# Splitting the returned denominators on GpSimd ahead of the bulk loads, in a one-core kernel that gates linear attention with a ReGLU block

## The chip, the cores and the metric

The kernel runs on one core of a Trainium2 chip. A core has five engines that run side by side: TensorE (PE in the profile; PEld is its weight load) multiplies matrices into PSUM, VectorE (DVE), ScalarE (ACT) and GpSimd (POOL) work elementwise, and SyncE (SP) issues DMAs. DMAs issued by SP and by GpSimd come from different queues and are carried by the same 16 DMA engines. Engines wait for each other by semaphores, and each engine works through its own instructions in order.

The metric is the device time of one execution in microseconds; lower is better.

## The reference

The output mixes two branches of the same input x (2048 tokens of width 576) by a sigmoid gate. Branch a is linear attention with 32 heads of 18 features, whose feature map is a softmax and a softmax of the negated value. Branch b is a ReGLU feed-forward of width 4608.

```python
q, k, v = x @ wqkv, split into 32 heads
phi(y) = concat(softmax(y @ w_phi), softmax(-(y @ w_phi)))
kv  = einsum("bhsf,bhsd->bhfd", phi(k), v)
z   = einsum("bhsf->bhf", phi(k))
num = einsum("bhqf,bhfd->bhqd", phi(q), kv)
den = einsum("bhqf,bhf->bhq", phi(q), z) + 1e-6
a   = (num / den) @ wo
b   = (relu(x @ W_gate) * (x @ W_up)) @ W_down
out = g * a + (1 - g) * b        # g = sigmoid(x @ gate_w)
```

All of it is fp32. The kernel multiplies in fp32r, a form of lower precision, and makes up for it by splitting operands: the high part is the value copied to fp32r, the low part is the value minus the high part, and a product is taken as high·high, high·low and low·high.

## The kernel before

**Stage 1, up to about 247 us.** The loop over 16 tiles of 128 tokens makes keys, values and queries. `softmax_parts` finds the maxima, exponentials and sums of a tile; `key_steps` and `query_steps` scale it (one half of `e` on DVE, the other on GpSimd, L209). `turn` transposes a tile of queries on PE (tile `ptr`), ACT copies it to `et`, and an SP DMA stores it in DRAM as `eT`; the last four tiles stay on chip. `gate_logits` takes the gate's exponential from a column of the values tile `vt` and then sets 11 columns of it to one by a memset on GpSimd (L295). The matmuls of `kv_step` sum phi(k)ᵀv.

Beside this the loop prepares operands of stage 3. At t = 8 `scaled_sums` begins: it loads four tiles `xb` of 128 × 3 × 512 (L330), multiplies each by the rows `sb` (L333) and forms four differences (L338), all on GpSimd, and SP stores seven results as `xt` (L327). It is a generator, and each turn of the loop takes three steps of it.

**Stage 2, about 247 to 392 us.** The queries are worked through in four blocks of 512 tokens. `BLOCKS = (3, 0, 1, 2)` gives their order, and "block 0" to "block 3" below mean places in it. For each block:

1. `fetch` loads its turned queries into `ph`, four DMAs of 594 KB (L426): blocks 0 and 1 need none or come by SP, blocks 2 and 3 come by GpSimd's queue. Token tiles 10 and 11 belong to block 3, and their `eT` is stored by GpSimd's queue first (L387).
2. `sums` multiplies `ph` by the summed kv (PE, L542), ACT copies the results to `R` and `og`, and small SP DMAs collect the denominators as `dn` (L548, L550).
3. `gather` moves other rows of `og` into `R` by SP DMAs (L561, L564).
4. `invert` takes the reciprocal of `dn` (L579), multiplies it by the gate rows `gT` (L580) and sends it to another layout by an SP DMA, `kt<-dn` (L582), 32 rows of 512.
5. `split_inverse` splits what came back into high and low, the tile `rd`: ACT copies (L588), DVE subtracts (L589).
6. `divide`, once for each of five row groups: PE spreads `rd` over rows by a matmul with the 0/1 matrix `spread` (L600), DVE multiplies `R` by it (L602), ACT and DVE split the result into `oh` and `ol` (L603, L604).
7. `first_out` (block 0) and `project_out` (others) multiply by wo on PE, and `rows_out` copies the rows and stores them (`att`, L755).

`gate_rows` copies the gates to `gx` on GpSimd (L569), transposes them on PE (L573), and ACT copies them to `gT` (L574). `load_operand` issues loads of `xr` by GpSimd's queue for stage 3, and `root_rows` stores `sb` by the same queue (L743).

**Stage 3, from about 392 us.** The feed-forward, with matmuls at L1084, L1124 and L1147. The change does not touch it.

**What sets the order.** Stage 2 is written inside `in_order(tc, nc, nc.tensor, nc.sync, nc.gpsimd)`: PE, SP and GpSimd execute in the order of the code there. DVE and ACT are ordered by the scheduler of the framework, except where `after` holds an instruction behind another. In stage 1 the scheduler orders all engines. Once made, each engine's order is fixed. Tiles come from pools, and a tile that reuses a buffer waits for the last reader of it.

Of the kernel before, what the change touches and what calls it, by code (L numbers as in the profile page):

```python
# [1 line left out]

# [5 lines left out]
F32 = mybir.dt.float32  # L8
# [75 lines left out]
def gated_mix_kernel(  # L84
# [27 lines left out]
    tt = nc.vector.tensor_tensor  # L112
# [180 lines left out]
    def gate_logits(t):  # L293
        nc.scalar.activation(gs[:, t:t + 1], VT[t][:, 0:1], AF.Exp, scale=-1.0)
        nc.gpsimd.memset(VT[t][:, 0:(NQ - 1) * GS + 1:GS], 1.0)  # L295
# [72 lines left out]
    def turn_all(t, bb):  # L368

        for b, ps in bb:  # L370
            for i, g in enumerate(QN[b]):
                nc.tensor.transpose(ps[:, i], flat(EQ[t])[:, QC[g]:QC[g] + QK], ident)  # L372
        for b, ps in bb:
            gg = QN[b]
            if t >= FIRST:
                o = PH[t // 4][:, t % 4]
            else:
                if t not in ET:
                    ET[t] = etp.tile([QK, NQ, P], F32, name="et")
                o = ET[t]  # L380
            nc.scalar.activation(o[:, gg.start:gg.stop], ps[:, :len(gg)], AF.Copy)
        TURNED[t] = TURNED.get(t, 0) + len(bb) - 1
        TURNED[t] = TURNED.get(t, 0) + 1
        if TURNED[t] == 3:
            EQ.pop(t)
            if t < FIRST:
                (nc.sync if t < FIRST - 2 else nc.gpsimd).dma_start(eT[t * QK:(t + 1) * QK], ET.pop(t).rearrange("p g t -> p (g t)"))  # L387
# [54 lines left out]
    xw = AR.enter_context(tc.tile_pool(name="xw", bufs=4, **R_))  # L442
# [13 lines left out]
    for t in range(2, NT - 2):  # L456
        if t in (6, 10):
            load_x(t // 4 + 1)
        if t == 8:
            whole(half_gates(0))  # L460
            sb = xw.tile([P, 2, TB], F32, name="sb", bufs=1)
            for i in range(2):
                on_all_rows(pv1.tile([P, TB], F32, name="pg", tag="pv1"), sb[:, i], i)
            first_half = scaled_sums(nc.gpsimd.tensor_tensor, 0, [xw.tile([P, 3, TB], F32, name="xb") for _ in range(4)], sb, 0, TB)
        for _ in range(3):
            next(first_half, None)
        if t == 12:
# [11 lines left out]
            spread = kt_p.tile([2 * H, 5, P], F32R, name="spread")  # L479
            ones = raw.tile([2 * H, 5, P], F32, name="ones", tag="raw")  # L480
# [73 lines left out]
    RD, OW = {}, {}  # L554
# [21 lines left out]
    def invert(b):  # L576

        dn = DN.pop(b)
        nc.vector.reciprocal(dn, dn)  # L579
        tt(out=dn, in0=gT[:, BLOCKS[b] * P:(BLOCKS[b] + 1) * P], in1=dn, op=MULT)  # L580
        d2 = kt_[:H, :TB]
        nc.sync.dma_start(d2, dn)  # L582

    def split_inverse(b):

        d2 = kt_[:H, :TB]
        rd = RD[b] = rb.tile([2 * H, TB], F32R, name="rd", bufs=1)
        nc.scalar.activation(rd[:H], d2, AF.Copy)  # L588
        tt(out=rd[H:], in0=d2, in1=rd[:H].bitcast(F32), op=SUB)  # L589

    def divide(b, k):
# [7 lines left out]
        ps = kv_bank(1 - k % 2 if b > 1 else 0)  # L599
        nc.tensor.matmul(ps[:n], spread[:, k, :n], RD[b], start=True, stop=True)  # L600
# [47 lines left out]
    with in_order(tc, nc, nc.tensor, nc.sync, nc.gpsimd):  # L648
# [41 lines left out]
        sums(0, (3, 2), (two[:, 0], two[:, 1]))  # L690
        sums(0, (1,), (kv_bank(2),))
# [3 lines left out]
        turn(FIRST - 2, 0, turned(kv_bank(0)))  # L695
        turn(FIRST - 2, 1, turned(kv_bank(1)))
        turn(FIRST - 2, 2, turned(kv_bank(0)))
# [10 lines left out]
        with after(tc, nc, nc.scalar, last_of(nc, nc.scalar)):  # L708
            split_inverse(0)
# [8 lines left out]
        gather(1, 4, 3, 2, 1, 0)  # L718
# [105 lines left out]
    pt = nc.gpsimd.tensor_tensor  # L824
# [85 lines left out]
    with in_order(tc, nc, nc.tensor, nc.sync, nc.gpsimd):  # L910
        x0, x1, x2 = (operand_ahead(i) for i in range(3))
        load_operand(0, 0, nc.gpsimd)
        load_operand(0, 1, nc.gpsimd)
        fetch(BLOCKS[3], nc.gpsimd)
# [8 lines left out]
        divide(1, 4)  # L923
        for m in range(5):
            first_out(0, (m,))
            rows_out(0, m, PW[m])
            if m == 1:
                divide(1, 3)
            if m == 3:
                divide(1, 2)  # L930
        sums(2, (1, 0), halves)
        gather(2, 4, 3, 2, 1, 0)
        divide(1, 1)
        divide(1, 0)
        for m in range(5):
# [4 lines left out]
            if m == 2:  # L940
                gather(3, 4, 3, 2, 1, 0)
            if m == 0:
                invert(2)
                split_inverse(2)
            else:
# [3 lines left out]
            if m == 2:  # L949
                whole(x0)  # L950
            if m == 4:
                divide(2, 0)
                invert(3)
                split_inverse(3)
# [569 lines left out]
def _layout(A_x, A_wqkv, A_w_phi, A_wo, B_W_gate, B_W_up, B_W_down, gate_w):  # L1524
# [33 lines left out]
    spread = np.zeros((2, H, 5, P), np.float32)  # L1558
# [8 lines left out]
    spread = spread.reshape(2 * H, 5, P)  # L1567
# [19 lines left out]
```

## Time and profile before

| | us |
|---|---|
| median of 3 runs (lowest to highest) | 1648.82 (1646.73 to 1649.28) |
| profiled execution | 1647.01 |
| its span, first to last instruction | 1644.9 |
| TensorE busy in it | 1592.0 |
| mean granted TensorE clock | 0.986 of full speed |

The profiled execution is one run with the hardware profiler. Its span is 2.1 us shorter than the time of that execution, and that time lies 1.8 us below the median of the runs. Rows of the profile name an instruction by engine, line, operation and tiles, written as output<-inputs; a line can be that of a helper. The view of waits lists who waited for whom: the total, how often, and the longest. "x4" at the end of a row is a count. In the timeline the first number is the start and the second the duration, and a bracket gives the idle time ahead of the instruction and what ended it. In the chain of waits each piece is the work or the transfer that the next step had to wait for.

### The profile page before, as it was taken

How to read it: one execution, taken by the hardware profiler on the slowest of the kernel's cores; microseconds unless marked ns; L12 is line 12 of the kernel's file. 1: busy time of each engine (PE TensorE's matmuls, PEld its weight loads, DVE VectorE, ACT ScalarE, POOL GpSimd, SP SyncE). 2: the span in 40 equal slices, each digit the busy share in tenths (PEclk: the TensorE clock that was granted, in tenths of full speed). 3: DMA queues.
4: the chain of work that ended last, by engine and by line, in shares of the span. 5: the costliest groups of instructions: out<-in, count | busy, mean ns of one | idle time of the engine just before them, and what ended most of it. 6: DMA issues, size and time to landing. Idle time of an engine off the chain costs nothing.

```text
span 1644.9 us, 20158 instructions
## 1 busy us (share of the span) xinstructions
PE 1592.0 (97%) x7823; PEld 1322.1 (80%) x7823; DVE 1198.4 (73%) x1852; ACT 562.9 (34%) x922; POOL 163.9 (10%) x234
## 2 busy tenths in 40 slices
PE   9998997788999999999999999999999999999998
PEld 8898995456888888888888887778888888888887
DVE  4998674356778777887777778667777677777777
ACT  4344334345333333333233234223232323223231
POOL 0128211000000000000000002111111111111110
PEclk9999998899999999999999999999999999999999
DMA  8154305527775566565554543554343434344342
GB/s 265 65 180 165 113 17 146 147 90 289 282 255 204 200 233 240 204 219 208 216 203 184 198 161 115 170 211 165 133 175 133 191 127 178 131 164 159 143 166 72
DMA packets 65306, 284.42 MB, mean 173 GB/s; under 512 B 6842, under 2 KB 17338, under 8 KB 56508
## 3 DMA queue, kind: packets, MB, share of 16 engines
q1 hardware_dynamic: 62764, 273.14, 45.6%
q0 software_dynamic: 1872, 8.97, 2.0%
q8 instruction: 61, 1.00, 0.2%
q10 hardware_dynamic: 576, 1.05, 0.2%
q14 instruction: 33, 0.27, 0.0%
HBM read 172.51 MB, written 109.21 MB: 171 GB/s over the span
## 4 chain that ended last, share of the span: by engine, by line
PE 84%; DVE 5%; DMA 5%; ACT 2%; issue 2%; SPq 1%; POOL 1%; POOLq 0%; ACTq 0%; DVEq 0%
PE cx L1084 27%; PE ca L1084 13%; PE pd L1124 12%; PE pd L1147 10%; PE cy L1084 7%; PE kv L175 2%; PE pq L175 2%; PE pm L1124 2%; PE pm L1147 2%; PE pk L175 2%; DMA kt<-dn 2%; DMA wdr<-wd 1%; DVE sm L204 1%; PE pv L237 1%; PE ptr L372 1%
## 5 line engine op out<-in xcount | busy, mean ns | idle before, releaser
L1191 ACT ACTIVATE hh<-g 128x512 fp32r<-128x512 f32 x195 | 120.2, 626 | 459.1 <-DVE g L1241 289.8
L1162 DVE TENSOR_TENSOR ac<-pd,ac 128x512 f32<-128x512 f32 x238 | 164.1, 689 | 145.4 <-PE pd L1147 145.3
L1084 PE MATMUL cx<-xo,wb 128*128 128x512 f32 x1008 | 250.9, 392 | 4.6 <-DVE u L1366 3.5
L1084 PE MATMUL cx<-xo,ws 128*128 128x512 f32 x1008 | 252.4, 390 | 2.9 <-ACT g L1245 2.1
L1084 PE MATMUL ca<-xo,ws 128*128 128x512 f32 x1008 | 252.0, 389 | 0.6 <-DMA ws<-wsd 0.6
L1084 PEld LDWEIGHTS cx<-xo,wb 128*128 128x128 f32 x1008 | 189.1, 189 | 46.8 <-DVE u L1366 4.3
L1084 PEld LDWEIGHTS cx<-xo,ws 128*128 128x128 f32 x1008 | 188.9, 188 | 43.7 <-ACT g L1245 3.4
L1084 PEld LDWEIGHTS ca<-xo,ws 128*128 128x128 f32 x1008 | 189.1, 188 | 40.3 <-issue 1.0
L1124 PE MATMUL pd<-hh,wd 128*128 128x512 f32 x576 | 200.7, 389 | 0.0
L1147 PE MATMUL pd<-hh,wd 128*128 128x512 f32 x476 | 185.2, 389 | 0.0
L1130 DVE TENSOR_TENSOR ac<-pd,ac 128x512 f32<-128x512 f32 x144 | 99.1, 688 | 105.4 <-PE pd L1124 102.9
L1196 DVE TENSOR_TENSOR hl<-g,hh 128x512 fp32r<-128x512 f32 x195 | 136.5, 700 | 1.9 <-ACT hh L1191 0.2
L1245 ACT ACTIVATE g<-cx 128x512 f32<-128x512 f32 x144 | 85.0, 590 | 128.0 <-PE cx L1084 127.9
L1124 PEld LDWEIGHTS pd<-hh,wd 128*128 128x128 f32 x576 | 108.1, 188 | 22.5
L1084 PE MATMUL cy<-xo,wb 128*128 128x512 f32 x504 | 125.9, 389 | 0.0
L1047 ACT ACTIVATE wd<-wdr 128x384 fp32r<-128x384 f32 (+1 forms) x106 | 62.3, 606 | 152.6 <-DMA wdr<-wd 152.6
L1124 PE MATMUL pd<-hl,wd 128*128 128x512 f32 x288 | 112.1, 389 | 1.0 <-ACT xo L810 1.0
L1084 PEld LDWEIGHTS cy<-xo,wb 128*128 128x128 f32 x504 | 94.6, 188 | 19.6
L1147 PEld LDWEIGHTS pd<-hh,wd 128*128 128x128 f32 x476 | 89.4, 188 | 18.6
L1147 PE MATMUL pd<-hl,wd 128*128 128x512 f32 x238 | 92.6, 389 | 0.0
L794 POOL TENSOR_TENSOR xo<-xr,xo 32x512 fp32r<-32x512 f32 x5 | 8.2, 1653 | 664.8 <-DVE xo L794 657.1
L1050 DVE TENSOR_TENSOR wd<-wdr,wd 128x384 fp32r<-128x384 f32 (+1 forms) x106 | 69.5, 670 | 5.5 <-ACT wd L1047 5.5
(248 smaller groups left out, 2586.3 us busy)
## 6 DMA issues: line engine op xcount, KB each, us to landing
wsd<-ws SPq DMA_DIRECT2D x34, 1280.0 KB
ws<-wsd SPq DMA_DIRECT2D x34, 1280.0 KB
wbd<-wb SPq DMA_DIRECT2D x34, 960.0 KB
wb<-wbd SPq DMA_DIRECT2D x34, 960.0 KB
wr<-wgu SPq DMA_DIRECT2D x36, 768.0 KB
wdr<-wd SPq DMA_DIRECT2D x36, 576.0 KB
eT<-et SPq DMA_DIRECT2D x10, 594.0 KB
xt<-xb SPq DMA_DIRECT2D x7, 768.0 KB
```

Source lines behind the costliest of these rows:

```text
L175: nc.tensor.matmul(ps, w, m, start=i == 0, stop=i == len(pairs) - 1)
L204: nc.vector.tensor_reduce(out=sm.rearrange("p h s -> p (h s)"), in_=e.rearrange("p h s f -> p (h s) f"), axis=AX, op=ADD)
L1047: nc.scalar.activation(o[:, 0], a, AF.Copy)
L1050: tt(out=o[:, 1], in0=a, in1=o[:, 0].bitcast(F32), op=SUB)
L1084: nc.tensor.matmul(ps, w, v, start=first and m == 0, stop=m == len(pairs) - 1, skip_group_check=True)
L1124: nc.tensor.matmul(ps, w, v, start=k == 0 and (i < 2 or first), stop=k == len(mms) - 1 and (i < 2 or last), skip_group_check=True)
L1130: tt(out=a, in0=ps, in1=a, op=ADD)
L1147: mm = lambda ps, w, v, a, z: nc.tensor.matmul(ps, w, v, start=a, stop=z, skip_group_check=True)
L1162: tt(out=a, in0=ps, in1=a, op=ADD)
L1191: nc.scalar.activation(h, src, AF.Copy)
L1196: tt(out=l, in0=src, in1=h.bitcast(F32), op=SUB)
L1245: nc.scalar.activation(a, ps, AF.Copy)
```

## The change

The change has these parts:

- **Halves.** `scaled_sums` for the first half of the tokens is made in two parts of 256 columns, with eight half tiles `xb` of 128 × 3 × 256, and each turn of the loop takes five steps instead of three.
- **Memset.** The memset of `vt` in `gate_logits` goes from GpSimd to DVE.
- **Gate rows.** `gate_rows` stands between the sums of block 0, ahead of the last turns of token tile 10, which now use three banks at once.
- **Return first.** `split_inverse` runs on GpSimd (a copy and a subtraction). The store of the turned queries of tiles 10 and 11, the `fetch` of blocks 2 and 3 and the operand loads stand in GpSimd's code after a split.
- **Place of the inversions.** Each `invert` stands right after the first gather (`gather(b, 4)`), the other gathers after it; `invert(1)` moves up from the fourth sum of block 2 to the third division of block 0, and blocks 2 and 3 move up likewise.
- **Upper partitions.** Blocks 1 and 3 use partitions 64 to 127 of `kt`, `rd` and `spread` (128 rows now, the 0/1 matrix four times), blocks 0 and 2 the lower ones. There is one tile `rd` for all.
- **Banks.** `project_out` alternates two PSUM banks over blocks 1 and 2 and four banks in block 3; two divisions of block 1 alternate banks.

```diff
-        nc.gpsimd.memset(VT[t][:, 0:(NQ - 1) * GS + 1:GS], 1.0)
+        nc.vector.memset(VT[t][:, 0:(NQ - 1) * GS + 1:GS], 1.0)
...
-            if t < FIRST:
-                (nc.sync if t < FIRST - 2 else nc.gpsimd).dma_start(eT[...], ET.pop(t)...)
+            if t < FIRST - 2:
+                store_turned(t, nc.sync)
...
-            first_half = scaled_sums(nc.gpsimd.tensor_tensor, 0, [xw.tile([P, 3, TB], F32, name="xb") for _ in range(4)], sb, 0, TB)
-        for _ in range(3):
+            halves = [[xw.tile([P, 3, TB // 2], F32, name="xb") for _ in range(4)] for _ in range(2)]
+            first_half = chain(*(scaled_sums(pt, 0, halves[c], sb[:, :, c * TB // 2:][:, :, :TB // 2], c * TB // 2, TB // 2)
+                                 for c in range(2)))
+        for _ in range(5):
...
     def invert(b):
         dn = DN.pop(b)
         nc.vector.reciprocal(dn, dn)
         tt(out=dn, in0=gT[:, BLOCKS[b] * P:(BLOCKS[b] + 1) * P], in1=dn, op=MULT)
-        d2 = kt_[:H, :TB]
-        nc.sync.dma_start(d2, dn)
+        nc.sync.dma_start(kt_[2 * H * (b % 2):][:H, :TB], dn)
 
     def split_inverse(b):
-        d2 = kt_[:H, :TB]
-        rd = RD[b] = rb.tile([2 * H, TB], F32R, name="rd", bufs=1)
-        nc.scalar.activation(rd[:H], d2, AF.Copy)
-        tt(out=rd[H:], in0=d2, in1=rd[:H].bitcast(F32), op=SUB)
+        if not RD:
+            RD.append(rb.tile([4 * H, TB], F32R, name="rd", bufs=1))
+        i = 2 * H * (b % 2)
+        d2, hi, lo = kt_[i:i + H, :TB], RD[0][i:i + H], RD[0][i + H:i + 2 * H]
+        nc.gpsimd.tensor_copy(hi, d2)
+        pt(out=lo, in0=d2, in1=hi.bitcast(F32), op=SUB)
...
         sums(0, (3, 2), (two[:, 0], two[:, 1]))
+        gate_rows()
         sums(0, (1,), (kv_bank(2),))
...
-        gate_rows()
-        fetch(BLOCKS[2], nc.gpsimd)
         final = query_steps(FIRST - 1, eng=nc.vector)
         next(final)
-        gather(0, 4, 3, 2)
+        gather(0, 4)
         invert(0)
-        gather(0, 1, 0)
+        gather(0, 3, 2, 1, 0)
+        split_inverse(0)
+        store_turned(FIRST - 2, nc.gpsimd)
+        fetch(BLOCKS[2], nc.gpsimd)
...
         divide(0, 2)
+        gather(1, 4)
+        with after(tc, nc, nc.vector, last_of(nc, nc.vector)):
+            invert(1)
+        gather(1, 3, 2, 1, 0)
+        split_inverse(1)
...
+        store_turned(FIRST - 1, nc.gpsimd)
         divide(0, 1)
...
+        fetch(BLOCKS[3], nc.gpsimd)
         load_operand(0, 0, nc.gpsimd)
         load_operand(0, 1, nc.gpsimd)
-        fetch(BLOCKS[3], nc.gpsimd)
         first_out(2, range(5))
         sums(2, (4, 5), halves)
         divide(0, 0)
-        invert(1)
-        split_inverse(1)
...
-        gather(2, 4, 3, 2, 1, 0)
+        gather(2, 4)
+        invert(2)
+        gather(2, 3, 2, 1, 0)
+        split_inverse(2)
...
-    ps = kv_bank(2) if m % 2 else pv1.tile([P, TB], F32, name="pw", tag="pv1")
+    i = 5 * (b - 1) + m + 1
+    i = i % 2 if b < 3 else i % 4
+    ps = pv1.tile([P, TB], F32, name="pw", tag="pv1") if i == 0 else kv_bank((2, 0, 1)[i - 1])
```

Three places show how the order of instructions moves. The first is GpSimd in stage 1, around the scaled operands: `xb` are the operands, `e` the softmax tiles that GpSimd scales, `r` and `sm` the factors of queries and keys. Before:

```order
L333 TENSOR_TENSOR xb<-xb,sb 128x1536 x3
L209 TENSOR_TENSOR e<-e,r 128x32x18
L333 TENSOR_TENSOR xb<-xb,sb 128x1536
L295 MEMSET vt 128x11
L338 TENSOR_TENSOR xb<-xb 128x1536 x2
L209 TENSOR_TENSOR e<-e,sm 128x32x18
L338 TENSOR_TENSOR xb<-xb 128x1536 x2
L209 TENSOR_TENSOR e<-e,r 128x32x18
```

After:

```order
L334 TENSOR_TENSOR xb<-xb,sb 128x768 x5
L210 TENSOR_TENSOR e<-e,r 128x32x18
L339 TENSOR_TENSOR xb<-xb 128x768
L334 TENSOR_TENSOR xb<-xb,sb 128x768
L339 TENSOR_TENSOR xb<-xb 128x768
L334 TENSOR_TENSOR xb<-xb,sb 128x768
L339 TENSOR_TENSOR xb<-xb 128x768
L334 TENSOR_TENSOR xb<-xb,sb 128x768
L210 TENSOR_TENSOR e<-e,sm 128x32x18
L339 TENSOR_TENSOR xb<-xb 128x768 x3
L210 TENSOR_TENSOR e<-e,r 128x32x18
L339 TENSOR_TENSOR xb<-xb 128x768 x2
```

Ahead of the second query scale (the second row with `r`) stood eight full passes; now fourteen half passes stand there, and two follow it.

The second place is GpSimd in stage 2, from the copy of the gates on. Before:

```order
L387 DMA eT<-et 108x1408
L569 COPY gx<-gates 128x512
L426 DMA ph<-eT 108x1408 x4
L387 DMA eT<-et 108x1408
L769 DMA xr<-xt 128x1536 x2
L426 DMA ph<-eT 108x1408 x4
L743 DMA sbd<-sb 128x512 x2
L769 DMA xr<-xt 128x1536
```

After:

```order
L575 COPY gx<-gates 128x512
L595 CAST rd<-kt 32x512
L596 TENSOR_TENSOR rd<-kt,rd 32x512
L391 DMA eT<-et 108x1408
L430 DMA ph<-eT 108x1408 x4
L595 CAST rd<-kt 32x512
L596 TENSOR_TENSOR rd<-kt,rd 32x512
L391 DMA eT<-et 108x1408
L430 DMA ph<-eT 108x1408 x4
```

The two pairs of `rd` rows are the splits of blocks 0 and 1; each waits for its `kt<-dn`, and the store and the bulk load come behind it. The operand loads follow the second bulk load, then the splits of blocks 2 and 3 with the stores of `sb` between them.

The third is SP at the second return. Before, `kt<-dn` of block 1 stood behind rows of block 2:

```order
L561 DMA R<-og 20x512 x4
L548 DMA dn<-og 24x1x128
L550 DMA dn<-R 8x1x128
L582 DMA kt<-dn 32x4x128
L548 DMA dn<-R 24x1x128 x2
```

After:

```order
L554 DMA dn<-R 24x1x128 x4
L570 DMA R<-og 14x512 x2
L587 DMA kt<-dn 32x4x128
L567 DMA R<-og 20x512 x4
L554 DMA dn<-og 24x1x128
```

It now stands ahead of four gathers of its own block and of all rows of block 2.

More of the change, by code (lines that the diff above doesn't have):

```diff
@@ L1 @@
 from contextlib import ExitStack, contextmanager
+from itertools import chain
 import concourse.bass as bass
@@ L552, in sums @@
                 PH.pop(BLOCKS[b])
[L554 removed]
+    RD, OW = [], {}
     def gather(b, *kk):
@@ L598, in divide @@
         oh, ol = OW[b]
-        ps = kv_bank(1 - k % 2 if b > 1 else 0)
-        nc.tensor.matmul(ps[:n], spread[:, k, :n], RD[b], start=True, stop=True)
+        ps = kv_bank(1 - k % 2 if b > 1 or b == 1 and k < 2 else 0)
+        half = slice(2 * H * (b % 2), 2 * H * (b % 2 + 1))
+        nc.tensor.matmul(ps[:n], spread[half, k, :n], RD[0][half], start=True, stop=True)
         r = R[:n, k]
```

45 lines of the change are left out of this document (17 added, 28 removed).

## The prediction

> **What bounds the kernel now.** I read the page first: its busy times and the chain of work that ended last.
>
> ```profile
> span 1644.9 us, 20158 instructions
> PE 1592.0 (97%) x7823; PEld 1322.1 (80%) x7823; DVE 1198.4 (73%) x1852; ACT 562.9 (34%) x922; POOL 163.9 (10%) x234
> ...
> PE 84%; DVE 5%; DMA 5%; ACT 2%; issue 2%; SPq 1%; POOL 1%; POOLq 0%; ACTq 0%; DVEq 0%
> ```
>
> TensorE (PE) is the bound: it is idle for 1644.9 − 1592.0 = 52.9 us. A change that leaves its work alone can give back only idle time, or time at a low clock. So I asked the view of waits what PE waited for, and cut the span into windows where it waited.
>
> ```profile
> PE kv L600 <- DVE rd L589: 18.8, 4, 10.8
> PE ptr L372 <- POOL vt L295: 4.4, 1, 4.4
> PE kv L573 <- POOL gx L569: 2.3, 1, 2.3
> ```
>
> ```profile
> 150.00:170.00 20.00, 15.64 (x119) 14.93 (x118) 16.44 (x17) 6.78 (x12) 15.79 (x10) 0.91 0.60 202
> 260.00:300.00 40.00, 32.28 (x127) 20.14 (x128) 14.83 (x29) 13.77 (x23) 7.33 (x13) 0.83 0.47 122
> 300.00:330.00 30.00, 17.73 (x57) 9.42 (x56) 8.80 (x15) 9.72 (x17) 0.00 (x0) 0.77 0.57 159
> 330.00:390.00 60.00, 53.75 (x217) 37.06 (x216) 28.61 (x42) 26.88 (x40) 1.67 (x3) 0.97 0.44 160
> ```
>
> The columns are length, busy time of PE, PEld, DVE, ACT and POOL, then the granted PE clock. PE's idle time is 4.4, 7.7, 12.3 and 6.2 us: 30.6 of the 52.9 us, all in the part that the change touches. The clock loses about busy × (1 − clock): 1.4, 5.5, 4.1 and 1.6 us, 12.6 in all. So 43.2 us is the most that can come back.
>
> The largest wait is for the divisors (rd): the inverted denominators go out by DMA into another layout (kt<-dn), are split in two, and only then spread by PE. The chain of waits has that DMA four times, once for each block:
>
> ```profile
> 266.36 10.95 DMA kt<-dn
> ...
> 302.89 11.05 DMA kt<-dn
> ...
> 335.40 2.41 DMA kt<-dn
> ...
> 354.65 3.19 DMA kt<-dn
> ```
>
> It moves the same 64 KB each time, in 11 us or in 2.4 to 3.2 us. GpSimd's timeline shows what lay beside the slow two: loads of 594 KB (ph<-eT), issued from 264.16 and from 296.42 us, ahead of the DMAs at 266.36 and 302.89.
>
> ```profile
> 262.87 0.74 POOL L387 DMA_DIRECT2D eT<-et  x1 [13.18 <-ACT et L381]
> ...
> 264.16 2.21 POOL L426 DMA_DIRECT2D ph<-eT  x4
> ...
> 296.42 1.70 POOL L426 DMA_DIRECT2D ph<-eT  x3
> ```
>
> ```profile
> ph<-eT POOLq DMA_DIRECT2D x8, 594.0 KB, 13.0
> ```
>
> PE stood still for the slow ones (rows of its timeline; the bracket is the idle time ahead):
>
> ```profile
> 278.82 0.66 PE L600 MATMUL kv<-rd,spread 64*64 64x512 f32 x1 [5.03 <-DVE rd L589]
> ...
> 296.94 1.93 PE L542 MATMUL po<-ph,kvm 108*64 108x512 f32 x6
> ...
> 315.36 0.69 PE L600 MATMUL kv<-rd,spread 64*64 64x512 f32 x1 [10.80 <-DVE rd L589]
> ...
> 331.11 1.93 PE L542 MATMUL po<-ph,kvm 108*64 108x512 f32 x6
> ```
>
> The two po rows are the first sums of blocks 2 and 3, which read the bulk loads.
>
> **The change, step by step.**
>
> *Scaled operands in halves (150–170).* PE's 4.4 us stall is for a query scale that stands behind the large multiplies on GpSimd:
>
> ```profile
> L338 POOL TENSOR_TENSOR xb<-xb 128x1536 f32<-128x1536 f32 x4 | 15.9, 3975 | 0.2
> L333 POOL TENSOR_TENSOR xb<-xb,sb 128x1536 f32<-128x1536 f32 x4 | 13.9, 3500 | 4.6 <-ACT sb L321 4.6
> L209 POOL TENSOR_TENSOR e<-e,r 128x576 f32<-128x576 f32 x14 | 17.4, 1240 | 55.1 <-DVE r L356 34.4 <-ACT ph L381 7.1 <-ACT vt L291 7.1
> ```
>
> By the order, that scale stood behind all 8 passes; now it stands behind 5 + 6 + 3 = 14 halves, or 7 passes. A half should cost half: from 576 to 1536 elements the time grows by 2.35 ns an element, so 768 take about 1.7 us, against 3.5 / 2. So the scale comes 3.5 to 4.0 us earlier, and 0.4 to 0.9 us of the stall stays; I take 0.7. That saves 3.7 us of idle time and, as the gap no longer cools the clock, 1.2 us of its 1.4. Of the DMAs, the loads of the halves are 8 instead of 4, and SP waits idle behind them; a store of turned queries (eT, at 147.99) now stands behind eight half stores on SP instead of four full ones:
>
> ```profile
> 14.12 3.55 SPq L330 DMA_DIRECT2D xb<-xs  x4
> 24.62 0.37 SPq L166 DMA_DIRECT2D xr<-xT  x1
> ...
> 147.99 0.32 SPq L387 DMA_DIRECT2D eT<-et  x1
> ```
>
> Twice 3.55 us from 14.12 still ends at 21.2. The eighth half store waits for the 12th half pass, about 5 us past 147.99; its buffer is needed when PE's stalled turn runs, near 158. Both are costed at nothing; without that cover the store could hold PE for 1 us. The memset that moves to DVE is a rival below.
>
> *The first return (260–300).* The gate rows' copy (gx) no longer stands behind the store eT at 262.87, and PE's transposes of it move between two sums: the 2.3 us wait goes. No bulk load is in flight now when kt<-dn goes out. That is about 1.4 us earlier, as the gate rows, for which DVE waited 1.76 us, are ready:
>
> ```profile
> 265.99 0.29 DVE L580 TENSOR_TENSOR dn<-kt,dn 128x128 f32<-128x128 f32 x1 [1.76 <-ACT kt L574]
> ```
>
>  It should take 2.4 to 3.2 us like the later two; I take 2.8. The split moves from ACT and DVE to GpSimd:
>
> ```profile
> L588 ACT ACTIVATE rd<-kt x4: 628/628/628, 277.3 to 357.9; 32x512 fp32r<-32x512 f32 x4
> L589 DVE TENSOR_TENSOR rd<-kt,rd x4: 680/681/682, 278.0 to 358.5; 32x512 fp32r<-32x512 f32 x4
> ```
>
> ```profile
> L794 POOL TENSOR_TENSOR xo<-xr,xo 32x512 fp32r<-32x512 f32 x5 | 8.2, 1653 | 664.8 <-DVE xo L794 657.1 <-ACT xo L810 7.6
> L569 POOL COPY gx<-gates 128x512 f32<-128x512 f32 x1 | 0.6, 632 | 0.0
> ```
>
> On GpSimd that is 0.6 us for the copy and 1.2 (the 576-element row) to 1.65 us for the subtraction, say 2.1 with the gap, against 1.3: 0.8 us longer per block. The divisors are ready at 266.4 − 1.4 + 2.8 + 2.1 = 269.9 us. PE arrived at 278.82 − 5.03 = 273.8; less the 2.3 us and the slow matmuls that followed it, it arrives near 269.5. So 0.4 us of the 5.0 remains. What is late next is the chain of one division, DVE, ACT, DVE, some 0.7 us each, that the slow clock had covered: 1.5 us.
>
> The bulk load of block 2 now follows the split. From its store at 262.87 to the end of the slow return at 277.3 it took 14.4 us, so it ends at 269.9 + 14.4 = 284.3. Its reader, at 296.94 before, comes at the least 7.7 − 1.9 + 4.0 = 9.8 us earlier and, with nothing left over, 7.7 + 5.5 = 13.2: at 283.7 to 287.1. A wait of 0 to 0.6, taken as 0.5. Window: 2.4 of 7.7 us stays, 5.3 saved; of the clock's 5.5 us, 4.0.
>
> *The second return (300–330).* The denominators were inverted long before they were sent:
>
> ```profile
> 289.31 0.95 DVE L579 RECIPROCAL dn<-dn 128x128 f32<-128x128 f32 x1
> ```
>
> The DMA waited on SP behind rows of block 2 until 302.89. Now it follows its multiply at once, and the upper partitions let the split go ahead while block 0 still uses its divisors. The small transfers of block 1, which feed it, lie beside block 2's bulk, so I let them land with it at 284.3. Then 1.2 us on DVE, 2.8 of DMA and 2.1 of split: 290.4. PE wanted them at 315.36 − 10.80 = 304.6; 13.2 us earlier is 291.4. So the 10.8 us goes. Two waits take its place. The reciprocal stands in DVE's queue ahead of block 0's next division, and waits there for the transfers: about 1.3 us of PE. Block 3's load, with the store of the last turned queries ahead of it, waits on GpSimd for the split, starts at 291 and by the same 14.4 us ends at 305.4, at the worst 310, since result stores share the time. Its reader, at 331.11 before, comes some 12 + 10.8 + 2.6 = 25.4 us earlier: 305.7. A wait of 0 to 4; I take 2. Window: 3.3 of 12.3 us stays, 9.0 saved; of the clock's 4.1 us, 2.6.
>
> *The rest (330–390).* Blocks 2 and 3 are inverted earlier, but block 2's small transfers now lie beside block 3's load and the operand loads behind it: 0 to 4 us late, taken as 1.5. Block 3's return gains its place but pays the 0.8 us of GpSimd: 1.4. Alternating the projection's banks over the blocks removes waits for evictions; part of that is given back where PE meets the weights of the next stage, whose loads don't move: 1.0. So 3.9 of 6.2 us stays, 2.3 saved, and the clock as now.
>
> **The sum.** Idle time 3.7 + 5.3 + 9.0 + 2.3 = 20.3 us, clock 1.2 + 4.0 + 2.6 = 7.8, together 28.1. The profiled execution took 1647.0 us (span 1644.9); 1618.9 follows. The median of the runs, 1648.8, lies 1.8 us above it: 1621.
>
> [...]
>
> **The rivals.**
>
> 1. *The bulk loads become the late party.* GpSimd holds block 3's load, two operand loads and a store behind its wait for the return. If block 2's load ends 3 us later and block 3's takes some 7 us more than PE can cover, 2.5 + 5 us of waits are added to mine and about 2 of clock: 1630 (1626 to 1637). For it: by the 13.0 us median the two loads had some 20 us in hand (264.16 + 13.0 to 296.94; 298.1 + 13.0 to 331.11), and have none now.
> 2. *The new collisions cost nothing.* The small transfers of blocks 1 and 2 slip past the bulk, so DVE, block 3's load and block 2's return are all on time. Then only about 5 us of idle time and 2 of clock stay of the 43.2: 36 us saved, 1613 (1609 to 1616). Against it: 10.95 against 2.41 us above. [...]
> 3. *The return is slow for another reason.* Should kt<-dn take 11 us for blocks 0 and 1 without bulk beside it, the first stall stays and the second shrinks to about 3.5 us; the loads, held back for both, then lie beside block 2's return, which costs about 10. Saved are 5 in the first stage, 2 at gx and 7; lost are 10 and some 2 of clock: 1647. Against it: both quick returns had no bulk load beside them.
> 4. *Slower: the memset on DVE.* It waits for ACT's copy of the values; on GpSimd that cost nothing.
>
> ```profile
> POOL vt L295 <- ACT vt L291: 30.2, 10, 7.0
> ```
>
> ```profile
> 119.57 0.40 ACT L291 ACTIVATE vt<-kv 128x294 f32<-128x294 f32 x1
> 119.70 1.35 DVE L204 TENSOR_REDUCE sm<-e 128x64 f32<-128x1152 f32 x1 [0.77 <-ACT e L201]
> ```
>
> If ten waits of 3.0 us fell on DVE ahead of the next softmax and passed to PE in full, the time would be 1621 + 30 = 1651. It decides from 2.8 us of PE time a wait, which eats the 28. Against it: the memset stands behind the L204 reduction, and the copy has landed (119.97) when that ends (121.05).
>
> **How the numbers follow.** The forecast has 0.55 (1615 to 1627 by its own bounds), rival 1 0.24, rival 2 0.13, rival 3 0.03, rival 4 0.05. From 1608 to 1637 all of the first three lie but their far ends; about 0.15 is left outside. A measurement of this kernel tells about 0.2%, 3.3 us, from no change. Forecast and rivals 1 and 2 are faster by more: 0.92; rival 3 counts as same, 0.03; rival 4 as slower, 0.05.
>
> **What would show it.** In the chain of waits all of the first two kt<-dn pieces should be near 3 us; PE's wait at the spreading matmul should fall from 18.8 to under 5 us; the clock in 260–300 should be above 0.9; GpSimd's first bulk load should be issued behind its rd subtraction; PE's 4.4 us at ptr should be under 1. The forecast is wrong if PE waits for ph by more than 4 us, if DVE's reciprocal of block 1 waits beyond 287 us, or if kt<-dn is still 11 us.

## The result

The changed kernel took 1625.46 us (median; 1623.44 to 1627.11), beside 1647.78 us for the kernel before: a ratio of 0.9864, with a 95% interval from 0.9847 to 0.9881. It is 22.3 us faster. The prediction said 1621 us, 1608 to 1637. The profiled execution took 1625.07 us, with a span of 1623.3.

### The profile after

The page's head and the shares of its chain of work, as shown of before:

```profile
span 1623.3 us, 20196 instructions
PE 1587.4 (98%) x7823; PEld 1319.7 (81%) x7823; DVE 1195.4 (74%) x1864; ACT 559.9 (34%) x918; POOL 171.7 (11%) x234
...
PE 88%; DVE 4%; DMA 3%; POOL 2%; ACT 1%; issue 1%; SPq 0%; DVEq 0%; POOLq 0%; ACTq 0%
```

PE is idle for 35.9 us where it was 52.9. What it waits for up to 420 us, apart from the start and the feed-forward:

```profile
PE kv L176 <- ACT oh L611: 4.6, 1, 4.6
...
PE kv L176 <- DVE ol L612: 1.9, 1, 1.9
PE ptr L373 <- POOL e L210: 1.5, 1, 1.5
...
PE po L548 <- DMA ph<-eT: 1.2, 1, 1.2
...
PE kv L608 <- POOL rd L596: 0.2, 1, 0.2
```

The 18.8 us of waits for the divisors (rd) are 0.2. In their place the two first rows are new: 6.5 us, at an output projection. The same windows as before, with the same columns:

```profile
150.00:170.00 20.00, 18.48 (x151) 17.76 (x151) 16.70 (x20) 8.52 (x13) 18.19 (x11) 1.00 0.62 192
...
260.00:300.00 40.00, 37.71 (x160) 21.42 (x158) 19.17 (x33) 16.26 (x28) 10.46 (x16) 1.00 0.65 175
300.00:330.00 30.00, 23.41 (x87) 13.30 (x87) 9.19 (x14) 12.42 (x21) 2.97 (x4) 0.89 0.41 143
330.00:390.00 60.00, 53.68 (x210) 40.53 (x209) 43.98 (x61) 30.43 (x43) 3.79 (x3) 0.94 0.68 249
```

The first two windows come near the forecast: they idle for 1.5 and 2.3 us, where 0.7 and 2.4 were left, and the clock is 1.00. In 300–330 us 6.6 us of idle time stay, and the clock is 0.89. The last window now holds the start of the feed-forward, so it can't be set against the old one.

Marks in the program can be compared better than times. PE's first and last value sums of stage 1, and its first feed-forward matmul, before and after (the two times in a row are the first and the last start):

```profile
L412 PE MATMUL kv<-e,vt x352: 256/256/301, 57.2 to 247.1; 128*55 128x108 f32 x161, 128*37 128x108 f32 x15
...
L1084 PE MATMUL cx<-xo,wb x42: 387/392/628, 392.5 to 439.3; 128*128 128x512 f32 x42
```

```profile
L416 PE MATMUL kv<-e,vt x352: 256/256/301, 60.2 to 244.6; 128*55 128x108 f32 x161, 128*37 128x108 f32 x15
...
L1091 PE MATMUL cx<-xo,wb x63: 387/389/770, 367.0 to 435.2; 128*128 128x512 f32 x63
```

Three rows of PE's timeline stand between them: the first spreading matmul, and the first sums of blocks 2 and 3, where the prediction showed 278.82, 296.94 and 331.11 us.

```profile
266.92 0.44 PE L608 MATMUL kv<-rd,spread 64*64 64x512 f32 x1 [0.16 <-POOL rd L596]
...
282.65 1.90 PE L548 MATMUL po<-ph,kvm 108*64 108x512 f32 x6 [1.16 <-DMA ph<-eT]
...
311.70 1.93 PE L548 MATMUL po<-ph,kvm 108*64 108x512 f32 x6
```

| stretch | before | after | gained |
|---|---|---|---|
| to the first value sum | 57.2 | 60.2 | −3.0 |
| to the last value sum | 189.9 | 184.4 | 5.5 |
| to the first spreading matmul | 31.7 | 22.3 | 9.4 |
| to block 2's sums | 18.1 | 15.7 | 2.4 |
| to block 3's sums | 34.2 | 29.0 | 5.1 |
| to the first feed-forward matmul | 61.4 | 55.3 | 6.1 |
| to the end of the span | 1252.4 | 1256.3 | −3.9 |

So 25.5 us were gained by the start of the feed-forward, and 3.9 given back in it.

All four returns are fast. SP's issues of them, and GpSimd's copies that waited for them:

```profile
262.53 0.69 SPq L587 DMA_DIRECT2D kt<-dn  x1
283.05 0.63 SPq L587 DMA_DIRECT2D kt<-dn  x1
...
311.63 0.63 SPq L587 DMA_DIRECT2D kt<-dn  x1
...
331.04 0.63 SPq L587 DMA_DIRECT2D kt<-dn  x1
```

```profile
264.92 0.60 POOL L595 CAST rd<-kt 32x512 fp32r<-32x512 f32 x1 [16.90 <-ACT og L552]
...
285.29 0.60 POOL L595 CAST rd<-kt 32x512 fp32r<-32x512 f32 x1 [15.53 <-DMA kt<-dn]
...
313.92 0.60 POOL L595 CAST rd<-kt 32x512 fp32r<-32x512 f32 x1 [20.12 <-DMA kt<-dn]
...
333.37 1.50 POOL L595 CAST rd<-kt 32x512 fp32r<-32x512 f32 x1 [11.49 <-DMA kt<-dn]
```

From issue to copy it is 2.4, 2.2, 2.3 and 2.3 us, where the first two took 11.

What is late in 300–330 us is something else. The chain of waits, ACT's timeline and PE's:

```profile
295.03 11.50 DMA att<-o
```

```profile
303.49 0.59 ACT L764 ACTIVATE b<-pw 64x512 f32<-64x512 f32 x1 [7.48 <-DMA att<-o]
303.99 0.62 ACT L611 ACTIVATE oh<-R 128x512 fp32r<-128x512 f32 x1
```

```profile
304.66 0.69 PE L176 MATMUL kv<-oh,wo 128*128 128x512 f32 x1 [4.61 <-ACT oh L611]
307.29 0.80 PE L176 MATMUL kv<-ol,wo 128*128 128x512 f32 x1 [1.95 <-DVE ol L612]
```

Block 0's output rows go out through four buffers (`tb`). The fifth group of rows needs two of them, one for the copy `b` and one for `o`, and has to wait until stores `att<-o` have landed. They now leave from 292.74 us, beside block 3's load (issued 287.78 to 292.7) and two operand loads (from 292.68 us). ACT stands at `b`, and the copy of a division (`oh`), which PE needs, stands behind it.

### The profile page after: what moved, and what is told of

It reads as the page before. It is cut to its first block, busy times and chain, and to the rows that moved or that the text cites. A ratio compares the mean times of both kernels' runs of the same rounds, so it can differ in the third digit from the quotient of the medians.

```text
span 1623.3 us, 20196 instructions
## 1 busy us (share of the span) xinstructions
PE 1587.4 (98%) x7823; PEld 1319.7 (81%) x7823; DVE 1195.4 (74%) x1864; ACT 559.9 (34%) x918; POOL 171.7 (11%) x234
## 4 chain that ended last, share of the span: by engine, by line
PE 88%; DVE 4%; DMA 3%; POOL 2%; ACT 1%; issue 1%; SPq 0%; DVEq 0%; POOLq 0%; ACTq 0%
PE cx L1091 27%; PE ca L1091 13%; PE pd L1131 12%; PE pd L1154 10%; PE cy L1091 7%; PE kv L176 4%; PE pq L176 3%; PE pk L176 2%; PE pm L1131 2%; PE pm L1154 2%; PE pw L176 1%; PE kv L416 1%; DMA wdr<-wd 1%; PE pv L238 1%; DMA ph<-eT 1%
## 5 line engine op out<-in xcount | busy, mean ns | idle before, releaser
L807 POOL TENSOR_TENSOR xo<-xr,xo 32x512 fp32r<-32x512 f32 x5 | 8.2, 1638 | 656.2 <-DVE xo L807 648.4
```

## The experiments

Each is an edit of the changed kernel. The medians, with the ratio to the kernel before and its interval:

| run | us | ratio |
|---|---|---|
| changed kernel | 1625.46 | 0.9864 (0.9847 to 0.9881) |
| six output buffers (o6) | 1619.79 | 0.9835 (0.9813 to 0.9858) |
| operand loads later (xr_late) | 1622.03 | 0.9845 (0.9827 to 0.9863) |
| both (o6_xr_late) | 1614.89 | 0.9802 (0.9785 to 0.9818) |
| both, remainders on GpSimd (best_rests) | 1618.19 | 0.9823 (0.9802 to 0.9843) |
| bulk loads first (bulk_first) | 1632.70 | 0.9915 (0.9890 to 0.9941) |
| block 1 inverted late (invert1_late) | 1626.82 | 0.9879 (0.9863 to 0.9895) |
| split by ACT and DVE (act_split) | 1627.85 | 0.9875 (0.9858 to 0.9891) |
| operands whole (fullxb) | 1628.54 | 0.9888 (0.9868 to 0.9909) |
| loads whole (wide_loads) | 1624.99 | 0.9866 (0.9845 to 0.9886) |
| memset on GpSimd (memset_pool) | 1626.23 | 0.9867 (0.9847 to 0.9886) |
| one range (one_range) | 1648.96 | 1.0008 (0.9998 to 1.0017) |
| one range, split later (one_range_late) | 1626.44 | 0.9869 (0.9849 to 0.9889) |

### Bulk loads ahead of the split

```diff
-        split_inverse(0)
         store_turned(FIRST - 2, nc.gpsimd)
         fetch(BLOCKS[2], nc.gpsimd)
+        split_inverse(0)
...
-        split_inverse(1)
...
         load_operand(0, 1, nc.gpsimd)
+        split_inverse(1)
```

> The changed kernel with GpSimd's bulk loads issued ahead of its splits in blocks 0 and 1 (block 1's split behind block 3's load and the two operand loads too); nothing else is moved. Theory A (a return is slow only beside bulk loads): kt<-dn takes about 11 us again for blocks 0 and 1 instead of some 2.4, PE waits 4 to 6 us at the first spreading matmul and 6 to 10 us at the second, the clock falls under 0.9 in 260 to 300 us, and the time is 1638 to 1645. Rival B (the gain came from the inversion sent ahead of the other gathers): the returns stay under 4 us and the time within 3 us of 1625.

1632.7 us, 7 above the changed kernel. Block 0's return is slow again, as theory A said, and PE waits for it longer than the 4 to 6 us expected. GpSimd's loads, the chain of waits and PE's timeline:

```profile
260.82 2.20 POOL L430 DMA_DIRECT2D ph<-eT  x4
```

```profile
262.84 10.78 DMA kt<-dn
```

```profile
275.67 0.68 PE L608 MATMUL kv<-rd,spread 64*64 64x512 f32 x1 [9.36 <-POOL rd L596]
```

The same 64 KB by the same code took 10.8 us beside the load and 2.4 without it. At block 1 the edit did not do what it was meant to: GpSimd's store ahead of the loads waited until 289.28 us, behind the return that SP had issued at 286.62, so nothing collided. That is why the time stays short of the 1638 to 1645 expected.

### Block 1 inverted late

```diff
-        gather(1, 4)
-        with after(tc, nc, nc.vector, last_of(nc, nc.vector)):
-            invert(1)
-        gather(1, 3, 2, 1, 0)
-        split_inverse(1)
+        gather(1, 4, 3, 2, 1, 0)
...
         divide(0, 0)
+        invert(1)
+        split_inverse(1)
```

> The changed kernel with block 1's inversion and split back at the place that they had before: its gathers are sent all at once, and reciprocal, return and split come behind block 0's last division, with GpSimd's loads for block 3 ahead of them. Theory A (this is the second of the two returns that the bulk loads slowed): that return takes about 10 us, PE waits 8 to 11 us at block 1's first spreading matmul with a clock of about 0.8 behind it, and the time is 8 to 12 us above 1625: 1635. Rival B (the stores att<-o near 300 us wait for the same loads anyway, so the wait only changes its name): within 3 us of 1625.

1626.8 us: not told apart from the changed kernel. Theory A's return and wait are there at about half the length expected, and another wait beside them (the chain, then PE's waits):

```profile
265.19 9.27 DMA dn<-R
...
291.24 5.54 DMA kt<-dn
```

```profile
PE kv L608 <- POOL rd L596: 5.2, 2, 5.0
PE pw L625 <- DVE ol L612: 4.8, 1, 4.8
```

The second is the one that the prediction had feared at this place: DVE's reciprocal of block 1, without the order that the change gives it, waits for small transfers (the 9.3 us of dn<-R above), and a division of block 0 stands behind it. But the loads for block 3 left from 275.8 instead of 287.8 us; ACT, which in the changed kernel waited 7.5 us for a store `att<-o`, waits for none from 290 to 325 us, and PE's 6.5 us wait was gone. Rival B holds: the wait changed its name. By the times the early return of block 1 is worth little while four buffers hold the stores. The trace leaves room for more: from the last value sum to the first feed-forward matmul this kernel takes 126.9 us, against 122.4 to 125.1 in four kernels that have the changed kernel's code there, and its profiled execution had reached the last value sum early, at 240.6 us.

### Six output buffers

```diff
-    tb_ = BS.enter_context(tc.tile_pool(name="tb", bufs=4, **L_))
+    tb_ = BS.enter_context(tc.tile_pool(name="tb", bufs=6, **L_))
```

> The changed kernel with six buffers instead of four for the output rows (tile o/b/sb of the pool tb). Theory A (the output stores are the new late party: att<-o takes 11.5 us beside block 3's loads, ACT's copy b<-pw waits for it at 303.49 us and holds the division behind it): the copy finds a free buffer, PE's waits of 4.6 and 1.9 us near 300 us go, and with the low clock behind them about 8 us: 1617 us, ratio to before 0.981. Rival B (the division of block 1 is late of itself, by its chain DVE, ACT, DVE or by the sums before it): the wait stays, at another instruction, within 2 us of 1625.

1619.8 us, and the two waits near 300 us are gone, so theory A is right on the cause; of the 8 us about 5.7 came. The rest went to the next late party, block 2's return (PE's waits, then the chain):

```profile
PE kv L608 <- POOL rd L596: 4.3, 2, 4.1
```

```profile
290.25 9.40 DMA dn<-R
...
299.67 7.55 DMA R<-og
...
308.58 2.19 DMA kt<-dn
```

The return itself took 2.2 us and goes out last. The small transfers ahead of it, of 9.4 and 7.6 us, now follow the bulk that GpSimd issued from 286.1 to 292.1 us.

### The operand loads later

```diff
         fetch(BLOCKS[3], nc.gpsimd)
-        load_operand(0, 0, nc.gpsimd)
-        load_operand(0, 1, nc.gpsimd)
...
         split_inverse(2)
+        load_operand(0, 0, nc.gpsimd)
+        load_operand(0, 1, nc.gpsimd)
```

> The changed kernel with its four buffers; the two operand loads xr<-xt (768 KB each) are issued by GpSimd behind the split of block 2 instead of right behind block 3's load. Theory A (att<-o is slow because of what GpSimd has in flight, and the operand loads are the larger part): the first output store lands in under 6 us, PE's waits of 4.6 and 1.9 us near 300 us shrink to under 2 together, 1618 to 1620 us. Rival B (block 3's load of 594 KB alone makes the store slow): the store still takes 9 us or more and the time stays within 2 us of 1625.

1622.0 us, between the two. The store on the chain took 7.5 us instead of 11.5, and PE waited 3.4 us instead of 4.6 with 0.2 instead of 1.95 behind it:

```profile
296.35 7.48 DMA att<-o
```

Both loads seem to matter: without the operand loads the store took 4 us less, and beside block 3's load alone it still took 7.5 us, which is between what theory A and rival B said.

> Six output buffers and the later operand loads together. With six buffers alone PE waited 4.1 us for block 2's divisors, behind a dn<-R of 9.4 us and an R<-og of 7.6 us on the chain. Theory A (these small transfers were slow beside the operand loads): both take under 4 us, the 4.1 us wait goes, and the time is 3 to 5 us under that of six buffers alone: 1615 us. Rival B (the wait is for block 3's load, or for the inversion's place in the order): the wait stays above 3 us and the time within 1.5 us of 1620; worse, the operand loads now slow block 3's return.

1614.9 us, the fastest kernel of this study: 10.6 us under the changed kernel, with an interval that lies below that one's. Theory A, with one miss, in the chain and in PE's waits:

```profile
292.83 9.43 DMA dn<-R
...
302.28 4.04 DMA R<-og
```

```profile
PE kv L608 <- POOL rd L596: 0.6, 2, 0.4
```

R<-og fell from 7.6 to 4.0 us and the wait went; dn<-R, which leaves while block 3's load is in flight, stayed at 9.4. The longest new wait of PE is 2.0 us for DVE, at a division near 327 us.

### Who splits

```diff
-        nc.gpsimd.tensor_copy(hi, d2)
-        pt(out=lo, in0=d2, in1=hi.bitcast(F32), op=SUB)
+        nc.scalar.activation(hi, d2, AF.Copy)
+        tt(out=lo, in0=d2, in1=hi.bitcast(F32), op=SUB)
+        nc.gpsimd.tensor_copy(RD[1][i:i + H], kt_[i:i + H, :1])
```

> The changed kernel with the split by ACT and DVE, as before, while GpSimd only reads one element of each row of the returned denominators, so that its bulk loads still wait for the return. Theory A (what helps is the order of the transfers, not the engine that splits): the divisors come some 0.6 us sooner, the bulk loads 1.3 us sooner, and the time is within 2 us of 1625. Rival B (a split on ACT and DVE makes these two wait for the return, with block 1's drains behind it): PE waits 2 us or more at the sums or divisions behind the return, 1628 or more.

1627.9 us. It lies 2.4 us above the changed kernel and the intervals overlap: neither theory is told apart by time. In the trace PE waits 1.7 instead of 0.5 us at block 0's first output, and 1.7 instead of 0.7 us at block 2's first, as B said, but no drain is held for long. Most of the gain is there without GpSimd's split, so the order of the transfers carries it.

### One range of partitions

```diff
-        nc.sync.dma_start(kt_[2 * H * (b % 2):][:H, :TB], dn)
+        nc.sync.dma_start(kt_[:H, :TB], dn)
...
-        i = 2 * H * (b % 2)
+        i = 0
...
-        half = slice(2 * H * (b % 2), 2 * H * (b % 2 + 1))
+        half = slice(0, 2 * H)
```

> The changed kernel with all blocks' denominators and divisors in the lower partitions, as before. Theory A (by the trace, block 1's split starts at 285.3 us, when block 0's last spreading matmul has just read the divisors, at 284.5 to 285.0): the split waits 0 to 1 us and the time is within 1.5 us of 1625. Rival B (the shared rows chain the blocks together: the split, and the bulk loads behind it, slip and PE waits for block 3's sums): PE's wait near 300 us grows by 3 us or more, 1629.

1649.0 us, no faster than the kernel before, and by neither theory. I had read the order from times, not from the code: the split of a next block is written ahead of the last divisions of the block before it. With one range these divide by the next block's divisors, so this kernel no longer computes the same result, and they wait for them:

```profile
PE kv L608 <- POOL rd L596: 29.3, 4, 10.5
```

So the second experiment writes each split behind the last division of the block ahead (with the edit above):

```diff
-        split_inverse(1)
...
-        store_turned(FIRST - 1, nc.gpsimd)
...
-        fetch(BLOCKS[3], nc.gpsimd)
...
         divide(0, 0)
+        split_inverse(1)
+        store_turned(FIRST - 1, nc.gpsimd)
+        fetch(BLOCKS[3], nc.gpsimd)
...
-        split_inverse(2)
         divide(1, 1)
         divide(1, 0)
+        split_inverse(2)
...
-                split_inverse(3)
...
                 divide(2, 0)
+                split_inverse(3)
```

> One range of partitions for all blocks' denominators and divisors, as before, with the split of each next block written behind the last division of the block ahead of it, so that every division has its own block's divisors; the bulk loads stay behind the split. Theory A (in the trace of the changed kernel block 0's last spreading matmul reads the divisors at 284.5 to 285.0 us and the split starts at 285.3; block 3's split at 333.4 stands ahead of block 2's last one at 338): nothing is lost at block 1, a wait of about 2 us appears ahead of block 3's first spreading matmul, 1625 to 1628. Rival B (the second range is what made the early return possible): PE waits 5 us or more at block 1 or at block 3's sums, 1632 or more.

1626.4 us, as theory A had it at block 1; the 2 us expected at block 3 did not come. The upper partitions let the split stand early in the order; they gave no time that these runs can tell.

### The halves, their loads and the memset

```diff
-            halves = [[xw.tile([P, 3, TB // 2], F32, name="xb") for _ in range(4)] for _ in range(2)]
-            first_half = chain(*(scaled_sums(pt, 0, halves[c], sb[:, :, c * TB // 2:][:, :, :TB // 2], c * TB // 2, TB // 2)
-                                 for c in range(2)))
-        for _ in range(5):
+            first_half = scaled_sums(nc.gpsimd.tensor_tensor, 0, [xw.tile([P, 3, TB], F32, name="xb") for _ in range(4)], sb, 0, TB)
+        for _ in range(3):
```

> The changed kernel with the scaled operands whole again, as before: four loads, eight passes of 128x1536 on GpSimd; the memset stays on DVE. Theory A (the halves save the 4.4 us wait at ptr and cost 2.4 us at the start): the wait at ptr is back at 4 us or more with a clock of about 0.9 in 150 to 170 us, the start is as before, and the whole is 2 to 3 us slower, 1628 us. Rival B (the halves cost nothing): 5 us slower, 1630. Rival C (the memset was what held GpSimd up): the wait at ptr stays under 2 us and the time within 1 us of 1625 or below it.

1628.5 us, 3.1 above the changed kernel, and its last value sum starts at 247.6 instead of 244.6 us. From its first value sum, at 58.7 us, that is 188.9 us, against 184.4. The old stall and the old clock are back (window, then PE's waits):

```profile
150.00:170.00 20.00, 15.60 (x118) 14.88 (x117) 16.72 (x18) 6.71 (x12) 16.39 (x8) 0.91 0.59 205
```

```profile
PE ptr L373 <- POOL e L210: 4.4, 1, 4.4
```

```diff
-        for i, a in enumerate(b):
+        for i, a in enumerate(b if wide is None else wide):
...
+            c1 = (2 * hf + t) * TB
+            nc.sync.dma_start(a, xs[:, k, :, c1 + c0:c1 + c0 + n] if wide is None else xs[:, k, :, c1:c1 + TB])
...
+            wide = [xw.tile([P, 3, TB], F32, name="xb") for _ in range(4)]
```

> The changed kernel, whose scaled operands are still computed and stored in halves, but loaded by four DMAs of full rows (xb<-xs) instead of eight of half rows. Theory A (the eight loads hold SP and the DMA engines longer, so the loads of x and of wq behind them land later, PE waits 2.3 us for wr<-wqT at 37.7 us and runs at a lower clock to 60 us): that wait goes, the last kv matmul of stage 1 ends 2 to 2.5 us earlier, 1623 us. Rival B (the 2.3 us are chance of one run): the time stays within 1 us of 1625, and the profile's place of the last kv matmul too.

1625.0 us: nothing. The loads themselves are as theory A said. SP's timeline of the changed kernel, and of this one:

```profile
14.20 8.89 SPq L331 DMA_DIRECT2D xb<-xs  x8
```

```profile
14.62 2.95 SPq L332 DMA_DIRECT2D xb<-xs  x4
```

The changed kernel's wait behind them,

```profile
PE psf L260 <- DMA wr<-wqT: 2.3, 1, 2.3
```

is gone, and a wait of 2.2 us for DVE stands there instead, as in the kernel before. The last value sum starts 1.0 us earlier, less than the chance of the first 60 us (below). So rival B holds by the times; that the wait is chance is less sure, as it is listed in eight of the eleven kernels with eight loads (0.3 to 2.3 us) and in none of the three with four.

```diff
-        nc.vector.memset(VT[t][:, 0:(NQ - 1) * GS + 1:GS], 1.0)
+        nc.gpsimd.memset(VT[t][:, 0:(NQ - 1) * GS + 1:GS], 1.0)
```

> The changed kernel with the small memset of each value tile on GpSimd again instead of DVE. Theory A (it costs nothing on either engine): within 1.5 us of 1625. Rival B (on DVE it waits for ACT's copy and delays the softmax, the slower rival of the prediction): faster than 1625 by 2 us or more. Rival C (on GpSimd it holds the halves up): the wait at ptr in 150 to 170 us grows from 1.5 to over 3 us, slower by 2 us or more.

1626.2 us, and 1.5 us at ptr as in the changed kernel: it costs nothing on either engine.

### The start of the feed-forward

On top of six buffers and later operand loads, in the two functions that prepare operands in place:

```diff
             low_in_place(0, i)
-            low_rest(0, i, tt)
+            low_rest(0, i, pt)
```

> Six output buffers, the later operand loads, and the 32-row remainders xo<-xr,xo of five operands at the start of the feed-forward on GpSimd instead of DVE. Theory A (DVE, busy without a gap from 364 to 384 us in the changed kernel, sets the start of the feed-forward): PE's waits of 3.5 and 1.1 us at cx<- shrink to under 3 together and the time is 2 us under 1615: 1613. Rival B (GpSimd, with 1.65 us an operation, is late itself, or the weights' loads are): 1615 or more.

1618.2 us: not better than without it, and the intervals overlap. PE's waits for DVE's `u` fell from 3.5 to 1.5 us and those for ACT's `g` rose from 1.1 to 4.2:

```profile
PE cx L1091 <- ACT g L1252: 4.2, 2, 4.0
```

From the first feed-forward matmul to the end of the span it takes 1254.4 us, against 1254.1 without this edit. DVE alone does not set that start. What does, ACT, the weights' loads or their order, stays open, and with it the 3.9 us given back there.

## Why the prediction was right, and where it was off

**The bound and the cause.** Right. Returns were slow because of bulk loads in flight; bulk_first shows it for the first return by restoring it (10.8 us beside the load, 2.4 without). For the second it rests on likeness: in no run does that return leave right behind the loads again, and in invert1_late, where it left some 8 us behind the operand loads, it took 5.5 us. Of the signs that the prediction named one failed, the wait at ptr. Rival 3, a return slow for another reason, falls. Rival 4 falls with memset_pool.

The terms below are set against the marks of the table above; idle times are those of the windows.

**Halves: forecast 4.9 us, measured 5.5 from the first value sum to the last.** The wait at ptr went from 4.4 to 1.5 us, not 0.7, the clock of that window went from 0.91 to 1.00, and about 1 us of smaller waits went too. With whole operands again (fullxb) 4.5 us of the 5.5 are lost, so mechanism and size are right. The stage as a whole gained only 2.5 us, because 3.0 were lost ahead of the first value sum, where I had costed the eight loads at nothing. The eleven kernels with eight loads start it between 55.6 and 61.4 us, the three with four at 57.2, 58.7 and 59.1: a cost of the loads can't be told from chance there.

**The first return: forecast 9.3 us, measured 9.4 + 2.4 = 11.8.** The return took 2.4 us (2.8 assumed), the split 0.60 and 1.26 (2.1 with the gap), the wait at the spreading matmul was 0.2 (0.4), that of the first output 0.45 (1.5), that for block 2's load 1.2 (0.5). 2.3 us of idle time stay, 2.4 were forecast. The clock is 1.00, where I had left 1.5 us of loss.

**The second return: forecast 11.6 us, measured 5.1. This is the term that failed.** In the window 300–330 the idle time fell by 5.7 us, not 9.0, and the clock's loss by 1.5, not 2.6. Neither of the leftovers that I named cost PE time. DVE did stand 6.6 us for the small transfers of block 1, which SP had issued by 271.4 us, beside block 2's load, and the division behind the reciprocal started only at 282.94 us:

```profile
281.74 0.95 DVE L585 RECIPROCAL dn<-dn 128x128 f32<-128x128 f32 x1 [6.57 <-DMA dn<-R]
```

But PE had other work, and waited for block 2's load until 282.65 us. For block 3's load PE did not wait. In their place stand 6.5 us behind an output store. I had asked what the moved loads would do to the parties that read them and to the returns, and not to the stores that leave at the same time through four buffers. It is rival 1's kind of case with another late party; six buffers confirm it, and invert1_late shows that this wait and the old one stand in for each other.

**Blocks 2 and 3 and the start of the feed-forward: forecast 2.3 us, measured 6.1 − 3.9 = 2.2.** Of the 3.9 us of waits that I had left, 1.0 stood for the start of the feed-forward. Ahead of its first matmul only 1.5 us stay (0.2, 0.7 and 0.6), and behind it 3.9 are lost. PE's early arrival alone does not explain that loss: the kernel with one range arrives at 389.9 us, 2.6 us ahead of the kernel before, and takes 1256.9 us from there to the end of the span, as the other versions take 1254 to 1257, against 1252.4 before. From that matmul on PE waits 4.2 us for ACT's `g`, against 2.1 before, while waits of 1.4 and 0.5 us for copies of output rows, which stood ahead of it, are gone. It looks as if the output banks moved part of the wait behind the mark; no run undoes the banks alone, so this is not shown. That the sum of the two came out as forecast may be luck.

**The sum.** 28.1 us forecast, 21.6 measured in the spans: 6.5 too much in the second return and 3.0 lost in the first 60 us; 0.6 too little in the halves and 2.5 at the first return; 0.1 too much in the rest. Part of the errors cancel, so the total is nearer than its terms deserve. The terms are those of one trace. From the last value sum to the first feed-forward matmul it has 122.4 us, and three kernels with the same code there (fullxb, wide_loads, memset_pool) have 123.1, 124.8 and 125.1.

Rival 2, that collisions cost nothing, is refuted by the transfers of 7.5 to 11.5 us seen beside bulk, though the three parties that it named, DVE, block 3's load and block 2's return, cost PE nothing in the changed kernel. Rival 1's load of block 3 was not late.

Undone one at a time, the halves are worth 3.1 us, the order at block 0 7.2, the order at block 1 1.4, the engine of the split 2.4. Of these only the order at block 0 is clear by the times, and the halves by the trace. About 8 of the 22 us are in no run of their own: the gate rows' copy, whose 2.3 us wait is gone, the early inversions of blocks 2 and 3, and the output banks were not undone singly.

## What to carry to other kernels

When a bulk load is moved out of the way of one small transfer, list every small transfer that leaves while it will be in flight, stores too, and count the buffers that wait for each. Here the wait changed its name: 10.8 us for the divisors became 6.5 us behind an output store. Then look again after each step: here two more buffers gave 5.7 us, the operand loads moved alone 3.4, and both together 10.6. An order read from times is no proof that the code could be written in another order.

## What the runs showed that was not expected

**DVE's subtraction took longer beside GpSimd's.** DVE's subtraction `ol<-R,oh` takes 0.69 us; where it meets GpSimd's split it takes up to 1.6. The views of that line, in the changed kernel and with the split on ACT and DVE (min, median, max in ns):

```profile
L612 DVE TENSOR_TENSOR ol<-R,oh x16: 670/684/1597, 272.5 to 346.3; 128x512 fp32r<-128x512 f32 x16
```

```profile
L614 DVE TENSOR_TENSOR ol<-R,oh x16: 673/688/693, 272.7 to 349.5; 128x512 fp32r<-128x512 f32 x16
```

```profile
285.98 1.28 POOL L596 TENSOR_TENSOR rd<-kt,rd 32x512 fp32r<-32x512 f32 x1
```

```profile
286.40 1.41 DVE L612 TENSOR_TENSOR ol<-R,oh 128x512 fp32r<-128x512 f32 x1 [0.70 <-ACT oh L611]
```

GpSimd ends at 287.26, and DVE 0.55 us later: it seems to have waited for GpSimd's end before its own work. The longest, of 1.60 us beside block 3's split, ends at 337.29, 0.54 us behind GpSimd's subtraction (334.96 to 336.75). GpSimd's copy of block 3 took 1.50 us instead of 0.60, beside DVE.

**The clock behind short waits.** In 260–300 us of the changed kernel it is 1.00 with four waits of 0.2 to 1.2 us, and in 300–330 us of the fastest kernel 1.00 with the wait of 2.0 us near 327 us. In act_split, with waits of 1.7, 0.3 and 0.4 us, it is 0.96 in 260–300 us. Before, with waits of 2.3 and 5.0 us in that window, it was 0.83. Behind the 2.3 us alone, with 0.35 and 0.25 us of waits close ahead of it, PE ran at 0.50 for about 3 us (0.62 on average in 264–266 us, 0.53 in 266–268). How long a wait must be to lower the clock is not shown.

**The first 60 us vary by themselves.** In the eleven kernels with eight loads of halves, whose code up to there differs in one of them by the memset alone, the first value sum starts between 55.6 and 61.4 us and the last between 240.6 and 246.2; from one to the other it is 184.4 to 185.1 us in all of them. The granted clock between 30 and 60 us goes with part of it: 0.94 at 240.6, 0.89 at 242.7, 0.77 to 0.84 at the others. A single trace's gain of 2 us at the end of that stage says nothing; the stretch between two marks in it, or the repeated times, do.
